# Order and gating of the first loads in a fused Fourier-mixing and squared-ReLU kernel

## The chip, the cores and the metric

The kernel runs on one core of one Trainium2 chip. The metric is the device time of one execution in microseconds; of the kernel before there are four timed runs, and the median is quoted. One execution more was taken by the hardware profiler, and the profile, the trace and their times are of that one.

## What is computed

```
X   = fft(fft(x, axis=1), axis=2).real      # x: 8 x 3008 x 256, f32
h   = max(X.reshape(24064, 256) @ w_in, 0)  # w_in: 256 x 2048
out = (h * h) @ w_out                       # w_out: 2048 x 256, out: 24064 x 256 f32
```

The real part of a two-dimensional Fourier transform of each of the eight batches goes through a feed-forward layer with a squared ReLU.

## The kernel before

**Transforms.** Both transforms are matrix products with sine and cosine tables. The one over the features (256) is folded into w_in: G1 and G2 are products of a 256-point cosine or sine matrix (`csD`) with w_in, G3 is G2 with signs (`gmat`, `gneg`). The one over the 3008 rows of a batch is done after folding: rows n, 1504 - n, 1504 + n and 3008 - n share sines and cosines, so they are first added and subtracted in pairs, and what remains are products with tables `cosT` and `sinT` (`stage1_first` for batch 0, `stage1_ops` for the others). They give `pt` and `qt` of a batch, from which PE makes h in chunks (`xb`, then ReLU and square on ACT and DVE) and then the second layer (`po`, with `wout`).

**x in the on-chip memory.** The tile `x4` has four slots. Slots 0 and 1 hold rows of the two halves of a batch in rising order, six rows (6 KB) for each of 126 partitions; SP loads them with plain transfers ("direct"). Slots 2 and 3 hold the mirrored rows, with the partitions in falling order; POOL loads them with indirect transfers ("gather"). Partition 126 holds the middle rows of the batch, repeated for each slot (`load_mid`: for batch 0 three small transfers on SP, one for slot 0, one for slot 3, one for slots 1 and 2). SP's transfers go through a hardware ring (q1 in the profile), POOL's through a software ring (q0).

**Batch 0.** It is loaded in row halves (`QH` = 3 of `NQ` = 6 rows). SP queues rows 0 to 2 of slots 0 and 1, then the middle rows, then rows 3 to 5 of both (L145, L127). POOL queues the gathers of slots 3 and 2, rows 3 to 5, then `jrow` (an iota, L149), then the gathers for rows 0 to 2 (L99). The fold of the first half needs direct rows 0 to 2, gathered rows 3 to 5 and the middle rows; the second half needs the others. For each half `fold_ops(0)` gives seven operations on DVE: two pair sums (`pair`, L360: `u` from `x4`), the first columns' sums (`pair0`, L364), the half sums (L369), the edges (L380) and two feature folds (L373).

**Queues around it.** The schedule is written out by hand: each engine and each queue works through its instructions in the order in which the program issues them. After the tables of batch 0, DVE makes four operations on `jrow` (`dmats`, L212 to L216) and a few vectors of signs; `fin` takes an absolute value (L202) and a copy (L221) on DVE and two sines on ACT; these give `csD`. Then SP issues the four quarters of w_in into `wst` (`load_w_in`, L760). `jrow` and the matrix that the sines read lie in the first of these four buffers, so the first quarter can only be issued when `fin`'s sines have been taken; in the trace that is at 10.12 us. Then come the mirrors of the tables on ACT and the folds of batch 0. After the first three operations of the second half's fold the loads of batch 1 are issued into the same `x4` (`load_x(1)`: L136, L132 on SP, L112 on POOL), and behind them on POOL the four quarters of w_out with a cast to f16 (`load_w_out`, L766). PE does six matmuls on zeros (`warm`), then the first half of stage 1, `gmat(0)` when the first quarter of w_in has been cast on ACT (L321), the second half of stage 1, and then the chunks. The scales `gE` are gathered from G2 by sixteen small transfers on SP (L558).

Of the kernel before, what the change touches and what calls it, by code (L numbers as in the profile page):

```python
# [24 lines left out]
def kernel(  # L25
# [7 lines left out]
    nc = tc.nc  # L33
    B, S, D = x.shape
    _, F = moe_w_in.shape
    P = 128
    M = S // 2
    QN = M // 2
    NQ = 6
    QH = NQ // 2  # L40
    NP = QN // NQ + 1
# [34 lines left out]
    def iota(name, shape, pattern, base, mult, dt=F32):  # L76
        t = const.tile(shape, dt, name=name)
        nc.gpsimd.iota(t, pattern=pattern, base=base, channel_multiplier=mult,
                       allow_small_or_imprecise_dtypes=True)
        return t  # L80
# [8 lines left out]
                   allow_small_or_imprecise_dtypes=True)  # L89

    x4 = xp.tile([P, 4, NQ, D], F32, name="x4")
    ez = const.tile([P, 2, NQ, P], F16, name="ez")

    def up(b, s, q=0, n=NQ):
        return bass.AP(tensor=x.tensor, offset=x.offset + (b * S + s * M + 1 + q) * D,
                       ap=[[NQ * D, NP], [1, n * D]])

    def gather_half(b, s, q):
        nc.gpsimd.indirect_dma_start(  # L99
            out=x4[0:NP, 2 + s, q : q + QH, :].rearrange("p q d -> p (q d)"),  # L100
            out_offset=None,
            in_=bass.AP(tensor=x.tensor, offset=x.offset,
                        ap=[[QH * D, B * S // QH], [1, QH * D]]),
            in_offset=bass.IndirectOffsetOnAxis(ap=idx3[0:NP, 0:1], axis=0),
            element_offset=(b * S + (s + 1) * M - NQ * NP + q) * D)
# [16 lines left out]
    def load_mid(b, eng):  # L122
        for s in range(2):
            row = x[b : b + 1, s * M : s * M + 1]
            if b == 0:
                for sl, n in (((0, 1), (3, 1)), ((1, 2),))[s]:
                    eng.dma_start(out=x4[NP : NP + 1, sl : sl + n].rearrange("p s q d -> p (s q) d"),  # L127
                                  in_=row.to_broadcast([1, n * NQ, D]))
            else:
                r = s * NQ + 1  # L130
                r2 = (3 - s) * NQ + NQ - 2
                eng.dma_start(out=xm[:, r : r2 + 1 : r2 - r], in_=row.to_broadcast([1, 2, D]))  # L132

    def load_x(b):
        for s in range(2):
            nc.sync.dma_start(out=x4[0:NP, s, :, :], in_=up(b, s))  # L136
            gather(b, 1 - s)
        load_mid(b, nc.sync)

    wst = [h2p.tile([P, 2, F // 4], F32, name="wst", tag="h2") for _ in range(4)]  # L140
    jm = wst[0].rearrange("p c f -> p (c f)")[:, 0 : 3 * P].rearrange("p (a b) -> p a b", a=3)
    for q in (0, QH):
        for s in range(2):
            gather_half(0, 1 - s, QH - q)
            nc.sync.dma_start(out=x4[0:NP, s, q : q + QH, :], in_=up(0, s, q, QH))  # L145
        if q == 0:
            load_mid(0, nc.sync)
            jrow = jm[:, 0]
            nc.gpsimd.iota(jrow, pattern=[[-1, P]], base=P - 1, channel_multiplier=0,  # L149
                           allow_small_or_imprecise_dtypes=True)  # L150
    idx = iota("idx", [P, 1], [[0, 1]], NP - 1, -1, I32)
    idx2 = iota("idx2", [P, 1], [[0, 1]], NQ // 2 * (NP - 1), -NQ // 2, I32)
    wout16 = const.tile([P, NFC, D], F16, name="wout16")
# [41 lines left out]
    def sgn_vecs():  # L195
        nc.gpsimd.tensor_scalar(out=sgn, in0=pidx, scalar1=P - 1.5, scalar2=None, op0=ALU.is_lt)
        nc.gpsimd.tensor_scalar(out=s3, in0=sgn, scalar1=-2.0, scalar2=None, op0=ALU.mult)
        nc.gpsimd.tensor_scalar(out=sgn, in0=sgn, scalar1=2.0, scalar2=-1.0, op0=ALU.mult, op1=ALU.add)
        nc.gpsimd.tensor_scalar(out=nsgn, in0=sgn, scalar1=-1.0, scalar2=None, op0=ALU.mult)
# [9 lines left out]
    def dmats():  # L209
        pv = nc.vector  # L210
        t, m = jm[:, 1], jm[:, 2]
        pv.tensor_scalar(out=m, in0=jrow, scalar1=pidx[:, 0:1], scalar2=None, op0=ALU.mult)  # L212
        pv.tensor_scalar(out=t, in0=m, scalar1=1.0 / D, scalar2=R23, op0=ALU.mult, op1=ALU.add)
        pv.tensor_scalar(out=t, in0=t, scalar1=R23, scalar2=-float(D),
                         op0=ALU.subtract, op1=ALU.mult)
        pv.tensor_tensor(m, m, t, op=ALU.add)  # L216
        nc.gpsimd.memset(csD[:, 0, 0, P - 1 : P], 1.0)

        def fin():
            absval(t, m)  # L220
            nc.vector.tensor_copy(csD[:, 0, 1, P - 1 : P], alt)  # L221
            act(csD[:, 0, 1, 0 : P - 1], m[:, 0 : P - 1], AF.Sin, bias=0.0, scale=wD)
            act(csD[:, 0, 0, 0 : P - 1], t[:, 0 : P - 1], AF.Sin, bias=hpi[:, 0:1], scale=-wD)

        def hi():
            act(csD[:, 1, :, 0:P:2], csD[:, 0, :, 0:P:2], AF.Copy, bias=0.0, scale=-1.0)
            nc.scalar.copy(csD[:, 1, :, 1:P:2], csD[:, 0, :, 1:P:2])
        return fin, hi
# [305 lines left out]
    for n in sizes:  # L534
        segs = []
        o = 0
        while o < n:
            b, i = divmod(g + o, NK)
# [214 lines left out]
    fe, fo = fold_ops(0)  # L753
    rd0, tr0, mi0 = table_ops(0)
    rd1, tr1, mi1 = table_ops(1)

    def load_w_in(*quarters):
        for c in quarters:
            cs = slice(c * F // 4, (c + 1) * F // 4)
            nc.sync.dma_start(out=wst[c],  # L760
                                in_=moe_w_in[:, cs].rearrange("(c p) f -> p c f", p=P))

    def load_w_out():
        for c in range(4):
            cs = slice(c * NFC // 4, (c + 1) * NFC // 4)
            nc.gpsimd.dma_start(  # L766
                out=wout16[:, cs, :],
                in_=moe_w_out[c * F // 4 : (c + 1) * F // 4, :].rearrange("(c p) o -> p c o", p=P))
# [13 lines left out]
    dmats_fin, dmats_hi = dmats()  # L782
    alt_vecs()
    sgn_vecs()
    for f in mi0[0:0] + [dmats_fin, lambda: load_w_in(0, 1, 2, 3)] + mi0[0:] + [dmats_hi] + fe[0]:
        f()
    for f in rd1[0:0] + fe[1][0:3] + [lambda: load_x(1)] + fe[1][3:]:
        f()
    load_w_out()
    for f in rd1[0:1]:  # L790
        f()
# [174 lines left out]
```

## Time and profile before

| what | value |
|---|---|
| timed runs, median (lowest to highest) | 604.95 us (603.0 to 605.7) |
| profiled execution, its own time | 603.21 us |
| its span | 601.3 us |
| PE busy | 579.2 us, 96% |
| ACT busy | 548.4 us, 91% |
| DVE busy | 523.0 us, 87% |
| POOL busy | 164.4 us, 27% |
| moved by DMA over the span | 56.24 MB, mean 94 GB/s |
| DMA share, 0 to 40 us, by windows | 0.72 to 1.6 from 1.5 us on |
| granted TensorE clock | 0.997 |

Times in the trace count from the start of the span. A DMA share is the time that packets took over that of 16 DMA engines; packets of two queues can overlap, so it can exceed 1. In a line of the timeline the first number is the start, the second the length, and what stands in brackets is the idle time of that engine ahead of the instruction and what ended it.

### The profile page before, as it was taken

How to read it: one execution, taken by the hardware profiler on the slowest of the kernel's cores; microseconds unless marked ns; L12 is line 12 of the kernel's file. 1: busy time of each engine (PE TensorE's matmuls, PEld its weight loads, DVE VectorE, ACT ScalarE, POOL GpSimd, SP SyncE). 2: the span in 40 equal slices, each digit the busy share in tenths (PEclk: the TensorE clock that was granted, in tenths of full speed). 3: DMA queues.
4: the chain of work that ended last, by engine and by line, in shares of the span. 5: the costliest groups of instructions: out<-in, count | busy, mean ns of one | idle time of the engine just before them, and what ended most of it. 6: DMA issues, size and time to landing. Idle time of an engine off the chain costs nothing.

```text
span 601.3 us, 12242 instructions
## 1 busy us (share of the span) xinstructions
PE 579.2 (96%) x4543; PEld 436.2 (73%) x4543; DVE 523.0 (87%) x959; ACT 548.4 (91%) x963; POOL 164.4 (27%) x156
## 2 busy tenths in 40 slices
PE   3779999999999999999999999999999999999997
PEld 1466677777777777777777778777787778877786
DVE  6799898998898998898898997899889899999880
ACT  7699899999989999989998989999998999999981
POOL 5301023122331122312023143422543423324400
PEclk9899999999999999999999999999999999999999
DMA  8996485574483414913233115133242231332112
GB/s 239 276 111 168 99 233 174 164 224 68 59 248 45 62 54 78 236 36 45 57 59 45 53 38 68 37 46 57 58 63 41 52 51 55 47 60 56 56 53 71
DMA packets 42232, 56.24 MB, mean 94 GB/s; under 512 B 7774, under 2 KB 36754, under 8 KB 42174
## 3 DMA queue, kind: packets, MB, share of 16 engines
q1 hardware_dynamic: 37310, 42.04, 33.4%
q0 software_dynamic: 4864, 13.44, 8.9%
q8 instruction: 35, 0.57, 0.4%
q14 instruction: 23, 0.19, 0.1%
HBM read 29.02 MB, written 24.64 MB: 89 GB/s over the span
## 4 chain that ended last, share of the span: by engine, by line
PE 90%; DMA 5%; ACT 1%; POOL 1%; issue 1%; DVE 1%; POOLq 0%; ACTq 0%; DVEq 0%
PE po L74 53%; PE xb L74 31%; PE pf L74 6%; DMA wout<-in_moe_w_out_dram 3%; DMA x<-in_x_dram,idx 2%; POOL x L99 0%; POOL x L112 0%; ACT h L747 0%; ACT os L618 0%; ACT h L726 0%; ACT bs L713 0%; POOL wout L766 0%; DVE bs L716 0%; DVE h L727 0%; DVE h L697 0%
## 5 line engine op out<-in xcount | busy, mean ns | idle before, releaser
L74 PE MATMUL po<-wout,h 128*128 128x256 f16 x3024 | 450.0, 272 | 2.7 <-DMA wout<-in_moe_w_out_dram 2.1
L74 PEld LDWEIGHTS <-h 128*128 128x128 f16 x3024 | 286.1, 98 | 112.6 <-issue 4.3
L74 PE MATMUL xb<-qt,G 128*128 128x512 f16 (+10 forms) x743 | 207.1, 321 | 1.7 <-ACT h L671 1.0
L714 POOL TENSOR_TENSOR bs<-bs,h 128x512 f32<-128x512 f32 x92 | 118.6, 1292 | 316.0 <-ACT bs L713 256.6
L727 DVE CUSTOM_DVE_ANT_0 h<-xb,bs 128x512 f16<-128x512 f32 (+1 forms) x231 | 144.8, 639 | 22.8 <-ACT h L726 22.0
L74 PE MATMUL xb<-pt,G 128*128 128x512 f16 (+16 forms) x512 | 146.3, 323 | 0.8 <-DVE h L727 0.4
L726 ACT ACTIVATE h<-xb 128x512 f16<-128x512 f32 (+1 forms) x218 | 135.4, 623 | 7.8 <-PE xb L74 5.5
L750 DVE TENSOR_TENSOR h<-h 128x2048 f16<-128x2048 f16 (+1 forms) x113 | 137.2, 1215 | 0.8 <-ACT h L738 0.7
L74 PEld LDWEIGHTS <-G 128*128 128x128 f16 x1255 | 120.2, 98 | 23.9 <-issue 3.2
L671 ACT ACTIVATE h<-xb 128x512 f16<-128x512 f32 (+1 forms) x166 | 104.1, 630 | 9.4 <-PE xb L74 8.4
L738 ACT ACTIVATE h<-xb 128x512 f16<-128x512 f32 (+2 forms) x155 | 96.0, 623 | 9.4 <-PE xb L74 7.8
L716 DVE SCALAR_TENSOR_TENSOR bs<-xb,h 128x512 f32<-128x512 f32 (+1 forms) x126 | 83.0, 660 | 18.1 <-PE xb L74 14.7
L748 ACT ACTIVATE h<-h 128x1024 f16<-128x1024 f16 (+1 forms) x79 | 84.8, 1074 | 0.0
L747 ACT ACTIVATE h<-h 128x1024 f16<-128x1024 f16 (+1 forms) x79 | 83.8, 1060 | 0.1
L697 DVE TENSOR_SCALAR h<-eb,gE 128x512 f16<-128x512 f16 (+1 forms) x198 | 70.1, 369 | 0.5 <-DMA eb<-qt 0.5
L618 ACT ACTIVATE os<-po 128x512 f32<-128x512 f32 (+1 forms) x95 | 59.5, 627 | 8.9 <-PE po L74 8.9
L713 ACT ACTIVATE bs<-xb 128x512 f32<-128x512 f32 x92 | 57.3, 623 | 3.2 <-PE xb L74 2.0
L112 POOL DMA_INDIRECT x<-in_x_dram,idx x16 | 21.0, 1315 | 77.9 <-DVE u L364 61.2
L360 DVE TENSOR_TENSOR u<-x 127x765 f16<-127x765 f32 x32 | 30.2, 965 | 3.2 <-DMA x<-in_x_dram,idx 3.2
L74 PEld LDWEIGHTS <-w 127*128 127x128 f16 (+1 forms) x192 | 22.2, 120 | 7.6 <-DVE w L373 1.8
L373 DVE TENSOR_TENSOR w<-v 127x384 f16<-127x384 f16 x64 | 22.2, 370 | 0.0
L74 PE MATMUL pf<-cosT,w 127*128 127x377 f16 (+1 forms) x96 | 20.7, 329 | 0.9 <-DVE w L373 0.9
(111 smaller groups left out, 212.6 us busy)
## 6 DMA issues: line engine op xcount, KB each, us to landing
out_dram<-os SPq DMA_DIRECT2D x157, 128.0 KB
x<-in_x_dram SPq DMA_DIRECT2D x14, 756.0 KB
wst<-in_moe_w_in_dram SPq DMA_DIRECT2D x4, 512.0 KB
eb<-qt SPq DMA_DIRECT2D x14, 128.0 KB
x<-in_x_dram SPq DMA_DIRECT2D x4, 378.0 KB
wout<-in_moe_w_out_dram POOLq DMA_DIRECT2D x4, 256.0 KB, 17.9
x<-in_x_dram,idx POOLq DMA_INDIRECT x20, 10.2
gE<-G SPq DMA_DIRECT2D x16, 0.2 KB
```

What stands on the lines that cost most here:

```text
L74: nc.tensor.matmul(o, l, r, start=start, stop=stop, skip_group_check=True)
L618: act(os_[:, js], po[:, js], AF.Copy, bias=0.0, scale=HS * HS)
L671: act(r_s(c, u), xb, AF.Relu, scale=-1.0)
L697: ts(out=X, in0=ebc[c][:, 0:n], scalar1=gE2[:, u : u + 1], scalar2=None, op0=ALU.mult)
L714: nc.gpsimd.tensor_tensor(T, T, X, op=ALU.add)
L716: stt(out=T, in0=xb, scalar=-2.0, in1=X, op0=ALU.mult, op1=ALU.add)
L726: act(r_s(c, u), xb, AF.Relu, scale=-1.0)
L727: mirrors.append((int(DEFER[c][u]), lambda: relu_d(c, u, lambda o, i: nc.vector._custom_dve(TENSOR_ADD_SAT, out=o[:, 0, :], in0=xb[:, 0, i ...
L738: relu_d(c, u, lambda o, i: act(o, xb[:, :, i], AF.Relu, scale=-1.0))
L747: act(h2[:, 0:nf], h2[:, 0:nf], AF.Square)
L748: rest.append(lambda: act(h2[:, nf:], h2[:, nf:], AF.Square))
L750: vt(h2, h2, h2, op=ALU.mult)
```

## The change

Three things are changed, all in the load of batch 0 and of w_in.

The two direct slots of batch 0 are issued as whole transfers (six rows, 6 KB for each partition) and first; the middle rows come behind them on SP. The gathers stay in row halves: rows 3 to 5 of slots 3 and 2, then rows 0 to 2, the order that they had before. `jrow` is now made after all four gathers.

All four quarters of w_in are issued by a new function, `w_gate`, which is called after the first three operations of the first half's fold (the two pair sums and the first columns' sums). It writes one element of each partition of each `wst` buffer with a memset on DVE, and then calls `load_w_in`, so that SP waits for DVE to have come that far.

```diff
-    def up(b, s, q=0, n=NQ):
-        return bass.AP(tensor=x.tensor, offset=x.offset + (b * S + s * M + 1 + q) * D,
-                       ap=[[NQ * D, NP], [1, n * D]])
+    def up(b, s):
+        return bass.AP(tensor=x.tensor, offset=x.offset + (b * S + s * M + 1) * D,
+                       ap=[[NQ * D, NP], [1, NQ * D]])
...
-    for q in (0, QH):
+    for s in range(2):
+        nc.sync.dma_start(out=x4[0:NP, s, :, :], in_=up(0, s))
+    load_mid(0, nc.sync)
+    for q in (QH, 0):
         for s in range(2):
-            gather_half(0, 1 - s, QH - q)
-            nc.sync.dma_start(out=x4[0:NP, s, q : q + QH, :], in_=up(0, s, q, QH))
-        if q == 0:
-            load_mid(0, nc.sync)
-            jrow = jm[:, 0]
-            nc.gpsimd.iota(jrow, pattern=[[-1, P]], base=P - 1, channel_multiplier=0,
-                           allow_small_or_imprecise_dtypes=True)
+            gather_half(0, 1 - s, q)
+    jrow = jm[:, 0]
+    nc.gpsimd.iota(jrow, pattern=[[-1, P]], base=P - 1, channel_multiplier=0,
+                   allow_small_or_imprecise_dtypes=True)
...
+    def w_gate():
+        for c in range(4):
+            nc.vector.memset(wst[c][:, 0, 0:1], 0.0)
+        load_w_in(0, 1, 2, 3)
+
...
-    for f in mi0[0:0] + [dmats_fin, lambda: load_w_in(0, 1, 2, 3)] + mi0[0:] + [dmats_hi] + fe[0]:
+    for f in mi0[0:0] + [dmats_fin] + mi0[0:] + [dmats_hi] + fe[0][:3] + [w_gate] + fe[0][3:]:
         f()
```

## The prediction

> **What bounds the kernel now.** I read the waits of PE first, because PE is busy for 96% of the span.
>
> ```profile
> PE warm L74 <- POOL ez L339: 9.3, 1, 9.3
> PE pc L74 <- ACT win L321: 3.4, 1, 3.4
> PE po L74 <- DMA wout<-in_moe_w_out_dram: 2.1, 3, 1.4
> PE pf L74 <- DVE w L373: 0.9, 1, 0.9
> PE xb L74 <- ACT h L671: 0.8, 2, 0.6
> ```
>
> These are PE's waits in the first 60 us (in total, times, longest). Over the whole span the list grows by little more than 1 us, and the table by stage has PE busy 20.00 of 20 us from 40 us on. So the time is set by the moment from which PE runs unbroken. The timeline of PE shows that moment.
>
> ```profile
> 37.29 0.60 PE L74 MATMUL po<-wout,h 128*128 128x256 f16 x4 [1.37 <-DMA wout<-in_moe_w_out_dram]
> 38.53 0.60 PE L74 MATMUL po<-wout,h 128*128 128x256 f16 x4 [0.43 <-DMA wout<-in_moe_w_out_dram]
> 39.91 0.60 PE L74 MATMUL po<-wout,h 128*128 128x256 f16 x4 [0.35 <-DMA wout<-in_moe_w_out_dram]
> ```
>
> PE stands still three times for the quarters of wout, last until 39.91. **The last late thing is a transfer**, and whatever moves its landing by d moves the end by d. A gain at PE's start that leaves wout alone is lost in these three waits. What carries wout is seen in the DMA view of four windows (queue, packets, MB, share of 16 engines; q1 is SP's hardware ring, q0 POOL's software ring): 0 to 4.4 us, 4.4 to 10, 15 to 19, 20 to 30.
>
> ```profile
> q1 hardware_dynamic: 252, 0.72, 53.1%
> ```
> ```profile
> q0 software_dynamic: 200, 0.87, 51.5%
> q1 hardware_dynamic: 313, 0.75, 39.1%
> ```
> ```profile
> q1 hardware_dynamic: 764, 1.48, 103.7%
> ```
> ```profile
> q1 hardware_dynamic: 367, 1.28, 58.1%
> q0 software_dynamic: 257, 1.04, 46.0%
> ```
>
> The two shares add up to about 100% from 7 us to 33 us. x of batch 0 (3.1 MB), w_in (2.1), x of batch 1 (3.1) and w_out (2.1) pass in a row, and DMA engines that stand idle for a moment give wout back later. The DVE timeline then gives the folds of batch 0.
>
> ```profile
> 8.13 1.47 DVE L360 TENSOR_TENSOR u<-x 127x765 f16<-127x765 f32 x1
> 10.79 0.96 DVE L360 TENSOR_TENSOR u<-x 127x765 f16<-127x765 f32 x1 [1.19 <-DMA x<-in_x_dram,idx]
> 11.66 0.18 DVE L364 TENSOR_TENSOR u<-x 127x6 f16<-127x6 f32 x1
> 14.95 0.96 DVE L360 TENSOR_TENSOR u<-x 127x765 f16<-127x765 f32 x1 [1.71 <-DMA x<-in_x_dram,idx]
> 16.16 0.95 DVE L360 TENSOR_TENSOR u<-x 127x765 f16<-127x765 f32 x1 [0.26 <-DMA x<-in_x_dram,idx]
> 17.04 0.18 DVE L364 TENSOR_TENSOR u<-x 127x6 f16<-127x6 f32 x1
> ```
>
> The pair sums of the first half end at 11.84 and of the second at 17.22; three of the four wait for a gather.
>
> **What the Trainium skill says.** "DMA: Bandwidth & Descriptors", Queues, rings and completion order: each DMA engine takes packets in turn from the rings that have work, and consumes one ring in order. The trace agrees as far as it goes: in 4.4 to 10 us the rings moved 0.87 and 0.75 MB side by side. So the middle rows, put behind two whole slots, come last of that ring. The same page, Issuing engines are not separate DMA queues: all queues share the same 16 engines, which is why I count bytes over both. "SBUF — State Buffer", SBUF: two separate sides: VectorE and GpSimd share a port pair by an exclusive lock, so a DVE operation in a two-port mode can be held by a POOL one. Here the DVE absolute value (L202) took 1.67 us from 7.93 beside POOL's memset of ez (1.40 us from 7.89); that fits, but nothing in the trace isolates it.
>
> **Part 1: whole slots first, middle rows last.** Removed: two of SP's four direct issues (0.33 to 0.54 us each) and the ring's dry spell after them: the late halves are issued only at 4.00, behind the middle rows, and the DMA share drops to 0.75 between 5 and 7 us (257 GB/s against 289 in the two us after). Added: the first half's sums now need both whole slots, 1.55 MB in place of 0.77, and the middle rows behind them. Before, 0.72 + 0.75 = 1.47 MB of that ring had passed by 10 us, of 1.57. The missing 0.10 MB at 0.75 / 5.6 = 0.134 MB/us takes 0.7 us; the dry spell given back is a quarter of 2 us, 0.5. So the ring, middle rows included, is through at 10.2, landed at about 10.5. The unknown is a packet's cost when rows are whole: bounded below by the rate of before (0), above by the whole-row loads of 20 to 30 us: 0.581 x 160 / 1.28 = 73 engine-us per MB against (37.4 + 35.0) / 1.47 = 49, so 24 x 1.55 = 37 engine-us. Spread over the 14 engines that the page's section Why a DMA increments its semaphore by 16 and not by 1 gives to 126 partitions, that is 2.6 us. I take 0, since in the later window other traffic ran too, and keep both ends.
>
> **Part 2: software ring.** Its four gathers keep their order (rows 3 to 5 of both slots, then 0 to 2); only jrow's iota (0.27 us at 4.84) goes behind all four. The third and fourth are issued 0.4 us earlier; jrow comes at about 7.6 and not 5.1. DVE's four operations on it (0.28 + 0.23 + 0.23 + 0.29) start at 7.7 and not 6.25 and end at 8.8, the sign vectors (0.7) at 9.5, absolute value and copy at 10.0. That beats 10.5, so x hides it. If POOL's memset of ez holds them by its whole 1.4 us, DVE is ready at 11.4 and the gate 0.9 later. ACT's sines of csD move by up to 1 us, hidden: ACT waits 3.6 us for w_in later.
>
> **Part 3: the gate.** Pair sums 10.5 to 11.5 and 11.5 to 12.4 (gather 2 landed at 10.8 before), their first columns (0.18) to 12.6, four memsets at 0.06 each with their starts to 12.9. Behind them on DVE stand half, edges and features, late by 0.3; behind the wait on SP only the loads of batch 1, which wait longer. w_in is issued at 12.9 and not 10.12. From SP's first issue at 0.73 to the first traffic about 1.0 us pass; I take 1.3 (1.0 to 1.7), so w_in flows from 14.2. x of batch 0 is through at 10 + (3.12 - 2.34) / 0.29 = 12.7. **For 1.5 us the engines have nothing.** Before, by 14.2, 2.34 + 0.74 + 1.2 x 0.25 = 3.38 MB had passed; after, 3.12. The missing 0.26 MB at w_in's own 0.37 MB/us is 0.7 us, and every later byte is late by that.
>
> **What comes earlier, and where it goes.** First w_in quarter: 14.2 + 0.52 / 0.37 = 15.6, landed 16.0; ACT's cast starts then and not at 17.38. Second half: 12.9 + 1.4 (half, edges, features, as 11.88 to 13.25 before) = 14.3, then 3.3 us (14.95 to 18.55 less 0.26 idle): 17.6 and not 18.55. PE's stage 1 ends 0.9 us early. Late next is wout: PE spends the 0.9 us waiting. The scales gE, on SP behind x, have DVE's use at 55.34, 13 us after their last issue: nothing.
>
> **Sum.** 0.7 us on the profiled execution: 603.2 + 0.7 = 603.9 (span 601.3, 1.9 around it). That execution is 1.7 below the median of the four, 604.95; on the median the sum is **605.7**.
>
> **Rivals.** (a) *Slower: the gate opens late.* Whole-row packets cost as at 20 to 30 us, the ring is through 2.6 us later, gate 15.5, w_in from 16.8. By 16.8 before had 3.38 + 0.2 + 1.8 x 0.37 = 4.25 MB: 1.13 MB missing, 3.0 us, 608.0. It decides from 0.67 MB (1.8 us), that is w_in from 15.3, middle rows 1.1 us later than I have them. For it: one last straggler of 14 engines holds everything. Against it: the ring no longer runs dry. (b) *Faster: the software ring gets ahead.* The second first-column sum ends at 16.2 and not 17.22, so batch 1's gathers and wout are issued 1.0 us earlier; if w_in's delay is borne by the hardware ring alone, wout lands 0.9 earlier, PE's 2.1 us of waits shrink by that: 604.0. Speaking against: both rings share engines that are full. (c) *Nothing:* from 33 us on the hardware ring moves almost nothing, it has slack, and wout lands as before: 604.95.
>
> **Chances.** Forecast 0.40 (605.0 to 606.7), (a) 0.35, (b) 0.12, (c) 0.13. About 0.3%, 1.8 us, is what a measurement of this kernel can tell from none. Faster by more: 0.05 out of (b). Slower by more: 0.32 out of (a) and 0.04 of the forecast's upper end, 0.36. Within: 0.59. The range runs from 603.8 (0.08 below, in (b)) to 608.3 (0.10 above: packets at their bound and the memset's hold together).
>
> **What would show it.** Right: pair sums from about 10.5, the second without a gap; memsets near 12.7; a dip in GB/s between 12.7 and 14.2; ACT's first cast near 16; PE's last wout wait ending 0.7 later. Part 1 is wrong if the first pair starts after 11.6; part 2 if DVE comes to it after x landed; the sum is wrong if wout's landing does not move with the dip, or if PE no longer waits for wout at all.

## The result and the profile after

| | median us (lowest to highest, runs) |
|---|---|
| before | 604.63 (602.23 to 607.09, 61) |
| after | 606.49 (604.45 to 608.16, 40) |
| ratio, 95% interval | 1.0030 [1.0022, 1.0037] |

The change costs 1.86 us, 0.3%. The forecast was 605.7, 0.7 over the median that was known then, and a range of 603.8 to 608.3: the sign is right and the time lies in the range, but the change costs over two and a half times what I worked out. The profiled execution after took 605.63 us with a span of 603.7; the one before took 603.21, so the two traces lie 2.4 us apart, more than the medians do.

The waits of PE, whole span (in total, times, longest), of the kernel after:

```profile
PE po L74 <- DMA wout<-in_moe_w_out_dram: 3.7, 1, 3.7
PE pf L74 <- DVE w L373: 3.1, 1, 3.1
PE pc L74 <- ACT win L321: 1.1, 1, 1.1
```

The wait for wout has grown from 2.1 to 3.7 us. The two waits below it, at PE's start, have changed places and add up to 4.2, where before they were 4.3 (3.4 + 0.9). PE's timeline shows where it stands:

```profile
35.40 0.27 PE L74 MATMUL xb<-qt,G 128*128 128x256 f16 x1
39.32 1.01 PE L74 MATMUL po<-wout,h 128*128 128x256 f16 x4 [3.65 <-DMA wout<-in_moe_w_out_dram]
40.55 1.06 PE L74 MATMUL po<-wout,h 128*128 128x256 f16 x4
42.17 0.60 PE L74 MATMUL po<-wout,h 128*128 128x256 f16 x4
```

PE comes to this wait 0.25 us earlier than before (the last product ahead of it began at 35.40, before at 35.65), so its start has lost nothing. It begins the third group 2.26 us later (42.17 against 39.91). wout's first quarter landed at 39.3 in place of 37.2 and its third at 41.6 in place of 39.9. The first two groups took 1.01 and 1.06 us in place of 0.60; the granted clock was lower there, see the last section.

The DVE timeline, for the folds of batch 0 and what stands ahead of them:

```profile
8.03 1.78 DVE L212 TENSOR_SCALAR wst<-wst,pidx 128x128 f32<-128x128 f32 x1 [1.70 <-POOL wst L149]
...
11.41 0.95 DVE L360 TENSOR_TENSOR u<-x 127x765 f16<-127x765 f32 x1
13.14 0.96 DVE L360 TENSOR_TENSOR u<-x 127x765 f16<-127x765 f32 x1 [0.78 <-DMA x<-in_x_dram,idx]
14.01 0.18 DVE L364 TENSOR_TENSOR u<-x 127x6 f16<-127x6 f32 x1
14.13 0.07 DVE L765 MEMSET wst<- 128x1 f32 x4
...
15.51 1.81 DVE L360 TENSOR_TENSOR u<-x 127x765 f16<-127x765 f32 x2
```

The first half's sums end 2.35 us later than before, the second half's (17.42) only 0.2. The four memsets overlap and take 0.07 us together. w_in is issued at 14.32:

```profile
14.32 1.95 SPq L760 DMA_DIRECT2D wst<-in_moe_w_in_dram  x4
```

The table by stage of the kernel after has the dip (us, busy time of each engine, then granted clock, DMA share, GB/s):

```profile
10.00:13.00 3.00, 2.26 (x6) 0.53 (x4) 2.22 (x11) 1.85 (x5) 0.75 (x4) 1.00 1.03 237
13.00:16.00 3.00, 0.62 (x3) 0.29 (x4) 2.74 (x11) 2.65 (x8) 0.00 (x0) 1.00 0.47 137
16.00:20.00 4.00, 2.88 (x11) 1.57 (x10) 3.34 (x8) 1.04 (x1) 1.98 (x2) 1.00 0.94 249
```

And of the kernel before, the same stretches:

```profile
10.00:13.00 3.00, 2.08 (x5) 0.45 (x3) 2.07 (x6) 3.00 (x9) 0.62 (x3) 1.00 1.05 246
13.00:16.00 3.00, 2.05 (x11) 1.21 (x12) 1.20 (x2) 0.82 (x4) 0.00 (x0) 1.00 1.01 282
16.00:20.00 4.00, 1.52 (x5) 0.65 (x5) 2.97 (x7) 1.64 (x2) 2.17 (x2) 0.86 1.01 366
```

From 13 to 16 us the kernel after moves 0.41 MB and the kernel before 0.85; from 16 to 20 it is 1.00 against 1.46. The dip is there, and it is followed by four slow microseconds that I had not foreseen.

### The profile page after: what moved, and what is told of

Its sections match the earlier page's. It is cut to its first block, busy times and chain, and to the rows that moved or that the text cites. A ratio compares the mean times of both kernels' runs of the same rounds, so it can differ in the third digit from the quotient of the medians.

```text
span 603.7 us, 12244 instructions
## 1 busy us (share of the span) xinstructions
PE 580.2 (96%) x4543; PEld 436.7 (72%) x4543; DVE 524.2 (87%) x963; ACT 548.2 (91%) x963; POOL 164.3 (27%) x156
## 3 DMA queue, kind: packets, MB, share of 16 engines
q0 software_dynamic: 4864, 13.44, 8.7%
## 4 chain that ended last, share of the span: by engine, by line
PE 88%; DMA 5%; ACT 4%; issue 1%; POOL 1%; DVE 1%; ACTq 0%; POOLq 0%; DVEq 0%
PE po L74 52%; PE xb L74 30%; PE pf L74 6%; DMA wout<-in_moe_w_out_dram 3%; DMA x<-in_x_dram,idx 2%; ACT h L726 1%; ACT h L747 1%; ACT h L748 1%; ACT os L618 0%; ACT bs L713 0%; POOL x L99 0%; POOL x L112 0%; DVE h L727 0%; DVE h L697 0%; DVE bs L716 0%
## 5 line engine op out<-in xcount | busy, mean ns | idle before, releaser
L738 ACT ACTIVATE h<-xb 128x512 f16<-128x512 f32 (+2 forms) x155 | 95.8, 622 | 11.2 <-PE xb L74 9.7
L716 DVE SCALAR_TENSOR_TENSOR bs<-xb,h 128x512 f32<-128x512 f32 (+1 forms) x126 | 83.1, 660 | 18.6 <-PE xb L74 15.3
```

Source lines behind the costliest of these rows:

```text
L716: stt(out=T, in0=xb, scalar=-2.0, in1=X, op0=ALU.mult, op1=ALU.add)
L738: relu_d(c, u, lambda o, i: act(o, xb[:, :, i], AF.Relu, scale=-1.0))
```

## The experiments

Theory A is the prediction's: between the end of batch 0's x and the start of w_in the DMA engines have nothing, and wout lands late by it. B puts the loss in the whole-slot loads themselves, C in the gate itself, D in the late `jrow`, E in PE's start. Each run is compared with the kernel before in its own series. The last two columns are of the run's trace, that is of one execution and not of the median: when w_in's first packet starts, and when PE begins its third group of products with wout.

| run | median us | ratio to before, 95% interval | w_in flows from, us | third wout group from, us |
|---|---|---|---|---|
| kernel before | 604.63 | 1 | 11.8 | 39.9 |
| changed kernel | 606.49 | 1.0030 [1.0022, 1.0037] | 15.4 | 42.2 |
| order only | 604.73 | 1.0000 [0.9986, 1.0013] | 13.0 | 40.5 |
| gate only | 604.63 | 1.0000 [0.9985, 1.0015] | 13.4 | 39.8 |
| half gated | 604.72 | 1.0000 [0.9985, 1.0016] | 13.0 | 41.3 |
| jrow early, first / second time | 605.47 / 605.22 | 1.0002 [0.9989, 1.0014] / 1.0001 [0.9988, 1.0014] | 14.6 / 14.0 | 42.3 / 40.3 |
| row halves in slot order | 605.54 | 1.0013 [0.9998, 1.0028] | 14.7 | 41.9 |
| changed kernel again | 606.07 | 1.0019 [1.0008, 1.0030] | 14.5 | 40.8 |
| gate late | 606.77 | 1.0035 [1.0022, 1.0049] | 15.9 | 43.0 |
| gate later still | 611.88 | 1.0115 [1.0096, 1.0134] | 17.9 | 47.3 |
| wout early, on before | 601.82 | 0.9947 [0.9934, 0.9960] | 12.2 | 36.5 |
| wout early, on after | 602.59 | 0.9963 [0.9951, 0.9974] | 15.1 | 37.4 |
| gate only with wout early | 601.47 | 0.9940 [0.9922, 0.9958] | 13.5 | 37.9 |

**Order only.**

```diff
-    for f in mi0[0:0] + [dmats_fin] + mi0[0:] + [dmats_hi] + fe[0][:3] + [w_gate] + fe[0][3:]:
+    for f in mi0[0:0] + [dmats_fin, lambda: load_w_in(0, 1, 2, 3)] + mi0[0:] + [dmats_hi] + fe[0]:
```

> The changed kernel without the gate: w_in is issued behind the sines of csD, as before. Theory A (the DMA engines stand idle between the end of batch 0's x and the start of w_in, and wout lands late by that): the sines end at 11.9 in the changed kernel, so w_in is issued at about 11.9 and not 14.3, there is no dip in GB/s between 13 and 16 us, wout lands within 0.7 us of before, and the time is 604.6 to 605.3. Rival B (whole slots hold back the software ring, and that is what is lost): 606.2 to 606.8, as in the changed kernel.

Measured: no change against before. w_in was issued at 11.97, as expected, though the loads of x and the late `jrow` are those of the changed kernel. B falls: the new order of the loads alone costs nothing that can be measured (by the interval at most 0.13%, 0.8 us). PE comes to wout early in this trace and waits long for it, and still nothing is lost; the length of the wait is not the price:

```profile
PE po L74 <- DMA wout<-in_moe_w_out_dram: 3.7, 1, 3.7
```

**Gate only**, put into the kernel before. The function `w_gate` is that of the change.

```diff
...
-    for f in mi0[0:0] + [dmats_fin, lambda: load_w_in(0, 1, 2, 3)] + mi0[0:] + [dmats_hi] + fe[0]:
+    for f in mi0[0:0] + [dmats_fin] + mi0[0:] + [dmats_hi] + fe[0][:3] + [w_gate] + fe[0][3:]:
```

> The kernel before with the gate alone. The first half's sums end at 11.84 there, so w_in is issued at about 12.1 in place of 10.12. Theory A: x of batch 0 then still runs to about 14.5, w_in flows from 13.2, hardly a dip, 604.6 to 605.3. Rival C (a gate costs by itself, wherever it opens, since w_in comes later): about as much as the whole change, 606.2 to 606.8.

Measured: no change either, so C falls. The DVE timeline of this run shows why; the gate opens at 11.9 and SP issues at 12.08:

```profile
8.13 1.51 DVE L360 TENSOR_TENSOR u<-x 127x765 f16<-127x765 f32 x1
10.90 0.95 DVE L360 TENSOR_TENSOR u<-x 127x765 f16<-127x765 f32 x1 [1.26 <-DMA x<-in_x_dram,idx]
11.78 0.18 DVE L364 TENSOR_TENSOR u<-x 127x6 f16<-127x6 f32 x1
11.90 0.07 DVE L765 MEMSET wst<- 128x1 f32 x4
```

PE waits for wout longer than before here too:

```profile
PE po L74 <- DMA wout<-in_moe_w_out_dram: 3.5, 2, 3.0
```

Neither half of the change alone shows a cost; together they cost 0.3%. The order moves the sums, and only the gate makes w_in depend on them.

**Half gated.** Two quarters of w_in behind the sines, two behind the gate.

```diff
     def w_gate():
-        for c in range(4):
+        for c in (2, 3):
             nc.vector.memset(wst[c][:, 0, 0:1], 0.0)
-        load_w_in(0, 1, 2, 3)
+        load_w_in(2, 3)
...
-    for f in mi0[0:0] + [dmats_fin] + mi0[0:] + [dmats_hi] + fe[0][:3] + [w_gate] + fe[0][3:]:
+    for f in mi0[0:0] + [dmats_fin, lambda: load_w_in(0, 1)] + mi0[0:] + [dmats_hi] + fe[0][:3] + [w_gate] + fe[0][3:]:
```

> The changed kernel with two quarters of w_in issued behind the sines (about 11.9) and only the other two behind the gate. Theory A: the ungated megabyte fills the dip between 13 and 16 us, so wout lands as before and the time is 604.4 to 605.2. Rival B (loss in the loads of x): 606.2 to 606.8.

Measured: as theory A says. With something for the engines to do in the dip, the loss is gone, although half of w_in still stands behind the gate. (wout's quarters landed at 38.3 to 42.3 in this one profile, so a single trace does not show what the median does.)

**Gate late.**

```diff
-    ... + fe[0][:3] + [w_gate] + fe[0][3:]:
+    ... + fe[0] + [w_gate]:
```

> The changed kernel with the gate behind the whole fold of the first half, four operations (1.3 us) later. Theory A: w_in is issued at about 15.6 and not 14.3, the dip is 1.3 us longer, wout lands 1.0 to 1.3 us later, 607.4 to 607.8. Rival B (the loss is in the loads of x): 606.3 to 606.7, unchanged.

Measured: 1.0035, above the changed kernel's 1.0030 by less than either interval; theory A's 607.4 is missed, and 606.77 lies just over the range of rival B. As a test between those two the run decides nothing. In this trace x came early and the gate opened at 14.85, so the delay against the changed kernel's two traces (14.32 and 13.44) is 0.5 and 1.4 us. PE comes late itself here, so its waits for wout are short, and it begins each group as wout lands, the third at 43.0:

```profile
PE pc L74 <- ACT win L321: 2.5, 1, 2.5
PE po L74 <- DMA wout<-in_moe_w_out_dram: 0.6, 2, 0.3
```

The run is worth more for its table by stage, in which the dip stands alone:

```profile
13.00:14.00 1.00, 0.00 (x0) 0.00 (x0) 0.88 (x3) 1.00 (x4) 0.00 (x0) 1.00 0.01 3
14.00:15.00 1.00, 0.49 (x2) 0.28 (x3) 0.98 (x8) 1.00 (x4) 0.00 (x0) 1.00 0.00 0
15.00:16.00 1.00, 1.00 (x5) 0.53 (x3) 1.00 (x2) 0.67 (x3) 0.00 (x0) 1.00 0.05 14
16.00:17.00 1.00, 1.00 (x4) 0.61 (x3) 0.97 (x3) 0.00 (x0) 0.11 (x1) 1.00 0.79 246
17.00:18.00 1.00, 0.93 (x4) 0.35 (x3) 0.96 (x5) 0.00 (x0) 1.00 (x1) 1.00 0.93 242
18.00:19.00 1.00, 0.00 (x0) 0.00 (x0) 0.58 (x1) 0.00 (x0) 0.70 (x2) 1.00 0.83 186
19.00:20.00 1.00, 0.00 (x0) 0.00 (x0) 0.00 (x0) 0.68 (x1) 0.99 (x2) 1.00 0.89 229
20.00:21.00 1.00, 0.58 (x3) 0.25 (x3) 0.00 (x0) 0.37 (x1) 1.00 (x2) 0.87 0.97 340
21.00:22.00 1.00, 1.00 (x4) 0.40 (x3) 0.00 (x0) 0.60 (x1) 1.00 (x3) 0.50 1.08 410
```

For three microseconds next to nothing moves (the last number of a line is GB/s). Then w_in has the engines to itself and still runs at 186 to 246 GB/s for four microseconds before it reaches 340 and 410.

**Gate later still.**

```diff
-    ... + fe[0][:3] + [w_gate] + fe[0][3:]:
+    ... + fe[0]:
...
-    for f in rd1[0:0] + fe[1][0:3] + [lambda: load_x(1)] + fe[1][3:]:
+    for f in rd1[0:0] + fe[1][0:3] + [w_gate, lambda: load_x(1)] + fe[1][3:]:
```

> The changed kernel with the gate behind the second half's first-column sum, so that w_in is issued at about 16.7 to 17.5. The start of w_in's flow against the loss so far: 11.8 none, 13.0 none, 13.4 none, 14.6 and 14.7 0.4 to 0.8, 15.4 1.9, 15.9 2.1. Theory A: flow from about 18, the dip is over 2.5 us longer than in the changed kernel, and since PE's start is then late as well it is paid in nearly full: 608.3 to 609.5. Rival B (the loss is in the loads of x or in a fixed cost of the gate): 606.3 to 607.

Measured: 7.0 us, far over theory A's upper end. PE's waits in this run say that another bound took over:

```profile
PE pc L74 <- ACT win L321: 4.8, 1, 4.8
PE pc L74 <- DVE pt L494: 4.2, 1, 4.2
```

w_in now mixes with batch 1's x, its last packet starts at 33.8 and not 23.8, and G itself is late. PE doesn't wait for wout any more: all of wout's quarters but the last land before PE begins its first group, at 45.2. So the loss does not grow along one slope. Up to the gate late it goes through the landing of wout; here wout is there first, and the delay goes through PE's own start.

**jrow early.** In the changed kernel `jrow` goes back between the two pairs of gathers.

```diff
...
     for q in (QH, 0):
         for s in range(2):
             gather_half(0, 1 - s, q)
-    jrow = jm[:, 0]
-    nc.gpsimd.iota(jrow, ...)
+        if q:
+            jrow = jm[:, 0]
+            nc.gpsimd.iota(jrow, ...)
```

> The changed kernel with jrow made between the two pairs of gathers, as before. Theory A: the second pair sum still waits for the second gather (landed at 13.1 in the changed kernel), so the gate opens at about 14.2 as in the changed kernel: 606.2 to 606.7. Rival D (the late jrow and the hold of DVE by POOL's memset set the gate): the gate opens 1 to 1.5 us earlier, 605.0 to 605.6.

Measured: 1.0002, where my theory said that nothing changes. I ran it again beside the changed kernel itself:

> The changed kernel itself once more, to stand beside the next one in the same series and to show how far the opening of the gate varies. By the earlier runs 1.4 to 2.3 us over the kernel before, whatever the theory. In every trace with the late jrow the first pair sum began at 11.4; here too. w_in is issued between 13.3 and 14.4, depending on the second gather.

> The changed kernel with jrow made between the two pairs of gathers, a second time beside the changed kernel. Theory A as first held (the second gather alone sets the gate): equal to the changed kernel within 0.3 us. Theory A with D (the late jrow holds DVE until 11.4 and the sums and so the gate open later; the dip is as long as both make it): 0.7 to 1.5 us faster than the changed kernel, 0.3 to 0.9 over the kernel before.

Measured: 1.0001 again, the changed kernel 1.0019 in the same series. So D is a part of the cause, though that rests on two series together: the two intervals of the second one overlap; against the 40 runs of the changed kernel (from 1.0022 on) both jrow runs lie lower (up to 1.0014). The DVE timeline of the second jrow run (its line numbers are one higher):

```profile
7.93 1.62 DVE L203 TENSOR_SCALAR wst<-wst 128x128 int32<-128x128 int32 x1
...
10.02 0.95 DVE L361 TENSOR_TENSOR u<-x 127x765 f16<-127x765 f32 x1 [0.47 <-DMA x<-in_x_dram,idx]
11.73 0.96 DVE L361 TENSOR_TENSOR u<-x 127x765 f16<-127x765 f32 x1 [0.76 <-DMA x<-in_x_dram,idx]
```

And of the changed kernel's second profile:

```profile
11.35 0.15 DVE L221 CAST csD<-alt 128x1 f16<-128x1 f32 x1
11.41 1.81 DVE L360 TENSOR_TENSOR u<-x 127x765 f16<-127x765 f32 x2
```

With the late `jrow` the first pair sum starts at 11.4 in all eight traces, straight after the copy, though the first gather has landed by then (9.6 to 11.2); without, it starts at 10.0 and 10.4, when the first gather has landed.

**Row halves in slot order.** Each whole slot as two transfers, so that packets are 3 KB again; `up` is the function of before.

```diff
...
     for s in range(2):
-        nc.sync.dma_start(out=x4[0:NP, s, :, :], in_=up(0, s))
+        for q in (0, QH):
+            nc.sync.dma_start(out=x4[0:NP, s, q : q + QH, :], in_=up(0, s, q, QH))
```

> The changed kernel with each whole slot issued as two row halves, in the same order (slot 0, slot 1, middle rows), so that packets are 3 KB again. In the changed kernel the software ring moved nothing between 4.4 and 6.7 us. If the size of the packets holds it back: it starts near 4.4 again, the first gather lands near 8.5 and not 11.2, the gate opens about 1 us earlier and the time is 605.3 to 606.0. If the amount queued ahead on the hardware ring holds it back: no change, 606.2 to 606.8; then the later middle rows may even add 0.3.

Measured: 1.0013 with an interval from 0.9998, between the two answers: inconclusive. In its trace the software ring again moved nothing from 4.4 to 6.7 us, beside 0.65 MB on the hardware ring, and the first gather landed at 10.5, between the 9.6 and 11.2 of the traces with whole slots. So in this trace the size of the packets is not what holds the software ring; what it does to the time stays open.

**wout early.** w_out's four transfers ahead of batch 1's gathers, behind memsets at the same place.

```diff
+    def wo_gate():
+        for c in range(4):
+            nc.vector.memset(wout16[:, c * NFC // 4, 0:1], 0.0)
+        load_w_out()
+
-    for f in rd1[0:0] + fe[1][0:3] + [lambda: load_x(1)] + fe[1][3:]:
+    for f in rd1[0:0] + fe[1][0:3] + [wo_gate, lambda: load_x(1)] + fe[1][3:]:
         f()
-    load_w_out()
```

> The kernel before with w_out's four transfers issued ahead of batch 1's gathers on the software ring, behind four memsets on DVE at the same place (the second half's first-column sum). Theory A (wout's landing sets the time): PE's 2.1 us of waits for wout go, 602.3 to 603.3. Rival E (PE's start sets the time, and the waits for wout only stand where it would otherwise wait for ACT): 604.3 to 605.

> The changed kernel with w_out ahead of batch 1's gathers in the same way. Theory A: PE's wait of 3.7 us for wout goes; as PE came to that wait 0.25 us earlier than in the kernel before, the two kernels are then equal, 602.3 to 603.3, within 0.5 us of the kernel before with the same edit. Rival E (the change costs at PE's start): it stays 1.5 to 2 us slower than the kernel before with the same edit.

Measured: 3.0 and 2.3 us below the kernel before, and PE waits for wout in neither. The changed kernel gains 3.9 us by this edit (606.49 to 602.59), about its own wait of 3.7. The 1.86 us between the kernels shrink to 0.8, and the intervals overlap. So most of the loss went through wout. E may keep a remainder: 0.8 is more than the 0.5 that A allowed, and in these two traces PE makes its first product for the chunks at 22.5 against 21.5. That this later start is what costs the 0.8 is not shown.

**Gate only with wout early**, the edits of both.

> The kernel before with the gate and with w_out ahead of batch 1's gathers: both kernels' edits that could be worth something, put together. With wout early the time hangs on PE's start. With the gate alone PE made its first product for the chunks at 20.75 and not 22.46. If that start is what counts once wout is early: 0.5 to 1.5 us below the kernel before with w_out ahead (601.8), 600.4 to 601.4. If ACT, busy without a gap from 22 to 36 us, counts: equal, 601.5 to 602.1.

Measured: 601.47, not to be told from 601.82. It is 0.6% [0.4%, 0.8%] below the kernel before, and nearly all of that is wout's place in the ring. The early start of 20.75 did not come about: in this trace PE makes its first product for the chunks at 22.4. So the run doesn't show what an earlier start is worth once wout is early.

## Why the prediction was right, and which terms were mis-sized

**The bound** was right: the landing of wout sets the moment from which PE runs unbroken. Moving wout forward took away the wait and the time with it. The traces show it a second way: in all fourteen the span ends 561.4 to 562.7 us after PE's third group with wout begins, while that beginning lies anywhere from 36.5 to 47.3 us. So what a kernel here gains or loses, it has by then, up to the 1.3 us by which the rests differ. The length of the wait tells little, since it grows when PE comes early: order only and gate only wait 3.7 and 3.5 us and lose nothing, gate late waits 0.6 us and loses 0.35%. One reading of the bound was too smooth: the DMA shares add up to about 100% only to 28 us; from 28 to 32 it is 1.20.

**Part 1** held for the hardware ring: 10.2 was forecast, and by 10 us it had moved 0.69 + 0.88 = 1.57 MB, all of it. What the step left out is the software ring beside it. I let the second gather land at 10.8 as before; it landed at 13.1 (11.2 to 12.8 in the other traces of this order). From 4.4 to 6.7 us the kernel after (first fence) has one queue alone, where before (second fence) it had two (packets, MB, share):

```profile
q1 hardware_dynamic: 111, 0.61, 89.3%
```
```profile
q0 software_dynamic: 86, 0.40, 56.9%
q1 hardware_dynamic: 128, 0.24, 31.0%
```

In the ten traces with the direct slots first the gathers' data flows from 6.6 to 7.1 us on, in the four with the order of before from 4.4 or 4.5 on. The issues on POOL are no later (1.90 and 3.83 us in both kernels), so it looks as if the gathers moved in the hardware ring's dry spell behind the middle rows and now wait until that ring has little left; that this is the reason is argued from the times, not shown. I had priced the dry spell as a loss that comes back; it was in use by the other ring.

**Part 2** is the step that failed: "absolute value and copy at 10.0. That beats 10.5, so x hides it." DVE was ready at 11.41, the upper bound that I had named (11.4), and the first gather had landed by then. In either order of `jrow` one DVE operation that runs beside POOL's memset of ez, and the three short memsets behind it, takes 1.6 to 1.8 us and ends at 9.6 to 9.8, when POOL is through with them. Before, that operation was the absolute value, and the copy and the first pair sum ended with it. Now it is the first of the four `jrow` operations; the other three, the sign vectors, the absolute value and the copy follow and take 1.6 us more. That fits what the Trainium skill says in "SBUF — State Buffer", SBUF: two separate sides (a lock held for a whole instruction); that it is this lock is not shown, since no run here takes the memsets away.

**Part 3.** w_in's issue at 12.9, measured 14.32 in the profile and 13.44 in the second one. In the second DVE's late start is all of it (0.9, less 0.4 by which my sums were too long); in the first the second gather adds 0.9. SP's issue to first packet, 1.3, was 1.05. ACT's first cast of w_in, which I had at 16.0, began at 18.80 (17.93 in the second profile).

**The missing bytes** were 0.26 MB in the forecast. In the profiles they are 0.22 by 10 us (2.34 against 2.12), 0.25 by 13, 0.69 by 16 and 1.15 by 20 us by the tables by stage above, since w_in starts slowly. The second profile of the changed kernel misses nothing by 10 and by 13 us, 0.42 by 16 and 0.80 by 20: the first 0.22 MB belongs to the one execution, the dip and the slow start to both (second profile):

```profile
10.00:13.00 3.00, 2.27 (x6) 0.53 (x4) 2.86 (x12) 1.84 (x5) 0.76 (x4) 1.00 0.91 235
13.00:16.00 3.00, 1.49 (x5) 0.81 (x6) 2.88 (x12) 2.66 (x8) 0.00 (x0) 1.00 0.45 139
16.00:20.00 4.00, 3.35 (x10) 1.46 (x9) 2.47 (x7) 1.05 (x1) 2.85 (x3) 1.00 0.90 271
```

The dip is also not the full stop that the forecast had: batch 0's x, forecast to be through at 12.7, was through at 15.4 and 13.9, and the DMA share from 13 to 16 us is 0.47 and 0.45.

But "every later byte is late by that" is wrong too, the other way: 1.15 MB at 0.37 MB/us would be 3.1 us, and wout's third quarter is only 1.75 late. From 20 to 30 us the kernel after moves 2.92 MB and the kernel before 2.33.

My sum came to 0.7 because its gate was 1.4 us too early (0.5 by the second profile), the slow start was not in it, and the catching up was not in it either. The last of these pulls against the other two, and the median before has come down by 0.3 us with more runs: that 606.49 lies so near to 605.7 is in part luck. By the table, with the gathers of batch 1 in their place, kernels with w_in flowing by 13.4 lose nothing, those from 14.0 to 15.4 lose 0 to 0.3%, and the later ones lose more. Inside the middle group there is no order to read: the changed kernel stands in it twice, with 14.5 and with 15.4.

**Second half and PE's start.** Forecast 17.6 for the second half's features, measured 18.75: the 0.9 us were not gained, so the change itself does not test whether they would be lost in the wait for wout. Order only and gate only do: PE makes its first product for the chunks at 20.9 and 20.8 in place of 22.5, waits longer for wout, and the median stays. **Rivals:** (a), the late gate, came about in part and by another way, not by slow packets but by the gathers and DVE; its decision point, w_in from 15.3, is where the profile stood, but its 608.0 was not reached. (b) and (c) did not happen.

## What to carry to other kernels

When transfers pass in a row and the last one is waited for, price a gate by the gap that it leaves between two of them, not by how long the gate itself waits: here two edits that show no cost alone cost 1.9 us together, because one moved the event on which the other made a load depend. Price a moved instruction with what now stands behind it on its engine, a lock by another engine included. And look first at the order on the ring that carries what is late: moving w_out ahead of loads that have time gained 3.0 us here, more than all of the change cost.

## What the hardware showed that I had not expected

- A ring whose gathers had been issued moved nothing from 4.4 to 6.7 us while the other moved 0.61 MB at 89% of the engines' time. The Trainium skill ("DMA: Bandwidth & Descriptors", Queues, rings and completion order) has each engine take turns between rings; in that stretch the trace does not show turns. Whether the gathers' descriptors were ready is not seen.
- In the gate late trace w_in starts at 186 to 246 GB/s for some 4 us, alone on the engines, and then DMA runs at 340 to 410. The gate is not needed for that: in order only it is 217 to 250 from 13 to 17 us and 367 in the next. In the kernel before, the slow part lay beside the tail of x (218 to 265 in all, 12 to 15 us). The cause stays open; no run isolates it.
- After the wait of 3.65 us PE's granted clock is 0.74 in the next stage, and four products take 1.01 to 1.06 us in place of 0.60. The third quarter landed 1.75 us later and was used 2.26 later, so about 0.5 us of the profiled loss is, by my estimate from these two, the clock. The Trainium skill's "TensorE: Matmul & The Clock Gate", What's actually happening, puts the drop after an idle window of about 3.4 us; here the wait of 2.6 us in the changed kernel's second profile already shows 0.65 and 0.92 in the stages around it (kernel after, then its second profile; the clock stands before the DMA share):

```profile
36.00:40.00 4.00, 0.68 (x4) 0.48 (x4) 3.96 (x10) 3.10 (x6) 0.00 (x0) 0.83 1.39 165
40.00:44.00 4.00, 4.00 (x29) 3.14 (x28) 2.14 (x9) 3.20 (x8) 0.00 (x0) 0.74 0.66 70
```
```profile
PE po L74 <- DMA wout<-in_moe_w_out_dram: 2.6, 1, 2.6
36.00:40.00 4.00, 2.07 (x10) 1.43 (x10) 3.83 (x9) 3.35 (x8) 0.00 (x0) 0.65 1.28 150
40.00:44.00 4.00, 4.00 (x34) 3.27 (x32) 2.67 (x10) 4.00 (x10) 0.00 (x0) 0.92 0.36 29
```

- x of batch 0, with nothing beside it, was through between 13.7 and 15.4 us in five traces of one and the same order of loads. A single profile of this start is good to about a microsecond, and two of them are no measure of a change of 0.3%.
